# A fused attention and Mish block: raw weight loads gated by an estimate of when their buffer was read, and the first correction rows turned and moved in one piece

## The chip, the cores and the metric

One core of one Trainium2 chip. The time is that of one execution on the device in microseconds (us); of several runs the median is given. The core has five engines with queues of their own, each of which runs its instructions in order: PE (matrix products), ACT (scalar functions, and copies out of the product banks), DVE (vector work), POOL (vector work in on-chip memory only) and SP (which here only issues transfers). A transfer is issued on one of these queues and then runs on 16 DMA engines. An instruction that waits holds everything behind it on its queue.

## The reference

```
xn = layernorm(x)                                      # x: 2048 rows of 512
q = (xn @ wq) as 32 heads of 16;  k = xn @ wk;  v = xn @ wv   # one key and value head for all
s = softmax(q k^T / 4) v, heads side by side, @ wo
h = xn @ w1 + b1                                       # 1792 hidden features
g = silu( (h * tanh(softplus(h))) @ w2 )
out = x + s * g
```

All arrays are float32, and the weights are drawn large, so the softmax is kept stable by subtracting the greatest score of each row.

## The kernel before

**Precision.** Products that need nearly full precision are made of three with operands that are split into a high and a low part (`mm12`, L645: 3 products for each 128 of the inner size). So each weight tile is loaded raw (`raw...`, 128x512), its high part is rounded out by ACT or POOL, and POOL subtracts to get the low part (`split`, L456). There are two raw buffers for all weights (`RAWS`, L424). The split form is then stored once to DRAM (`keep`, L475) and loaded again ready made for later row blocks. `ws` names the tiles of w1, `wb` those of w2 and wo, `wq` those of wq; in the lead-in the first `ws` tiles live in `xtw`.

**Work.** The rows are done in four blocks of 512 (`c`). A query step `v` is a group of four heads of one block: 32 steps. For each, a first set of score products `m` (L1054), 64 of them, is reduced by DVE to the greatest score of each row (L1058, `mb`). From these `c_rows` (L1070) makes two correction rows in four parts: `reduce` (L1077), `parts` (L1080 and L1082), `turn` (a transpose, L1087) and `move` (eight small transfers, L1097), which put the rows into the query tile `qt`. Then the score products `e` (L1025) come out with the maximum already subtracted, ACT takes the exponential (L1030, `pts`) and PE multiplies by the values (L1112, `pv`). Between these, the products of the other matrices run in groups of 12 or so into a bank `xps`: projections of q (copied out at L723 as `qf`), the hidden layer (L778, `hb`, then three ACT functions and POOL products into `act`), and the second layer and wo (`wbs`).

**Order.** The whole order is written out by the program, without any automatic scheduling. The main part runs in steps: 16 for each `v`, four `e` each, and four steps form a unit with one `xps` group (L653) in half-height products (L116). The lead-in, before the first `e`, is a small planner (L1393 to L1474): tasks with an engine, an estimated duration and dependencies are taken in the order of their estimated start, with clocks `T` for each engine. The main part is expected to begin at `E0` = 81 us of this plan. Where PE has nothing ready, the planner puts in pieces of an `xps` group at full height (L112) or a warming product (`warm`, L1348). `c_rows(0)`, the rows of the first query step, is three DVE tasks and an SP task there (L1433 to L1444).

**Loads.** `load` (L491) queues the raw load of the next tile on SP as soon as fewer than two raw tiles are taken in the plan, and `split` gives a raw tile free when the split has been written into the order (`raws[0] -= 1`, L468). `pool_at` and `busy` hold the planner's estimate of when POOL is done with what was given to it, and `step_of` turns it into steps. A load that is queued into a raw tile waits on SP until POOL's subtraction has read it.

**Key moves.** The keys of block c are copied, their low part made (L169, `ks`), and half of them are moved to the other partitions by `k_move` (L349, transfers at L351). The first score products against these keys wait for that.

Of the kernel before, what the change touches and what calls it, by code (L numbers as in the profile page):

```python
# [122 lines left out]
def block_kernel(ctx: ExitStack, tc: tile.TileContext, x, wq, wk, wv, wo, w1, b1, w2, out):  # L123
# [21 lines left out]
    def step_of(us):  # L145
        return base[0] + (us - base[1]) / STEP_US
# [34 lines left out]
    def f(ap):  # L181
        return ap.bitcast(F32)
# [199 lines left out]
    for j in range(4):  # L382
        o = slice(DH * j, DH * (j + 1))
# [38 lines left out]
    RING = {"wq": 1, "ws": 2, "wb": 5, "wx": 4}  # L422
    NRAW = {"wq": 1, "ws": 1, "wb": 1, "wx": 1}
    RAWS = 2  # L424
    raws = [0]
    items = {t: [] for t in RING}
    todo = {t: [0, 0] for t in RING}
    queue = deque()
# [27 lines left out]
    def split(tag):  # L456
        k = todo[tag][0]
        it = items[tag][k]
        w = home(tag, k)
        if not lead:  # L460
            busy[0] = max(busy[0], us_of(it.step + 1))
        if lead:
            act.activation(w[:, 0], it.raw, AF.Copy)
        else:
            hi_pool(w[:, 0], it.raw)
        sub(pool, w[:, 1], it.raw, f(w[:, 0]))
        it.tile, it.ready = w, pool_at(0.2)
        raws[0] -= 1  # L468
        todo[tag][0] += 1
        keep(it)  # L470

# [19 lines left out]
    def load(tag):  # L491
        its = items[tag]
        k, n = todo[tag]
        if tag == "wx" and m1_done.get((NC - 2, NFT - 1)) is None or lead and tag == "wq" and n > 1:
            return
        if n == len(its):
            return
        it = its[n]
        if taken(tag, n) and (tag != "ws" or kept.get(it.key)):
            return  # L500
        if n == k and kept.get(it.key):
            it.tile = home(tag, n)
            sp.dma_start(f(it.tile), kept[it.key])
            it.ready = math.ceil(2 * (sp_at(0.5) + 1.6)) / 2
            todo[tag][:] = n + 1, n + 1
        elif n - k < NRAW[tag] and raws[0] < RAWS:
            r = sb.tile([P, D], F32, tag="raw", name=f"raw{tag}{n}", bufs=RAWS)
            if len(it.src.shape) == 3:
                sp.dma_start(r.rearrange("p (t n) -> p t n", t=NDT), it.src)
            else:  # L510
                sp.dma_start(r, it.src)
            it.raw, it.step = r, (lead["arrive"]() if lead else sp_at(0.45))
            raws[0] += 1
            todo[tag][1] += 1

    def pump():
# [553 lines left out]
    def c_rows(v):  # L1070

        mp = sb.tile([P, 2, 3, 8], F32R, tag="mp", name=f"mp{v}", bufs=2)
        mx = f(mp[:, :, 0])
        w = {}

        def reduce():
            dve.reduce_max(out=mx, in_=mb_of[v].rearrange("p b (a z) -> p a z b", a=2), axis=AX.X)  # L1077

        def parts():
            dve.tensor_reduce(out=mp[:, :, 1], in_=mx.rearrange("p a (z o) -> p a z o", o=1), axis=AX.X,  # L1080
                              op=ALU.max, negate=True)
            dve.tensor_reduce(out=f(mp[:, :, 2]), in_=f(mp[:, :, 0:2]).rearrange("p a s z -> p a z s"), axis=AX.X,  # L1082
                              op=ALU.add, negate=True)

        def turn():
            cr = w["cr"] = sb.tile([P, 32], F32, tag="cr", name=f"cr{v}", bufs=2)
            dve.transpose(cr, f(mp[:, :, 1:3]).rearrange("p a s z -> p a (s z)"))  # L1087

        def move():
            q, cr = qt_of[v], w["cr"]  # L1090
            if not lead:
                sp_t[0] = max(sp_t[0], us_of(step[0]) + 4.0)
            for a in range(1, -1, -1):
                r = 64 * a + 48
                for b in range(4):
                    sp_at(0.68)
                    (act if lead and b % 2 else sp).dma_start(f(q[r:r + 2]).rearrange("o p (t b n) -> b o (p t) n", b=4, n=32)[b],  # L1097
                                 cr[32 * b + 16 * a:32 * b + 16 * a + 16])
        return reduce, parts, turn, move

# [105 lines left out]
    now = [0.0]  # L1206
# [15 lines left out]
    def task(eng, us, fn, deps=(), **kw):  # L1222
        t = Task(eng, us, fn, deps, **kw)
        plan[eng].append(t)
        return t
# [161 lines left out]
                   for d in k.deps)  # L1387

    begun = [0]
    rows = []  # L1390
    cdone = [None]
    kind = [None]
    while True:  # L1393
# [7 lines left out]
        b = best("PE")  # L1401
# [13 lines left out]
        s, e, k = min(opts, key=lambda o: o[0])  # L1415
# [5 lines left out]
        if k == "M":  # L1421
# [11 lines left out]
            if vdone[0] == 0 and got[0] == 32 and m_next[0] == m_next[1]:  # L1433
                vdone[0] = 1
                r = c_rows(0)
                r0 = task("DVE", 0.26, r[0])
                rp = task("DVE", 0.3, r[1], [r0])
                r1 = task("DVE", 0.25, r[2], [rp])
                rows[:] = [r0, rp, r1]

                def move():
                    r[3]()
                    cdone[0] = now[0] + 2 * 0.65 + 2.0
                task("SP", 2.6, move, [r1])  # L1444
        elif k == "X":
            fresh = cur["g"] is None
            if cur["g"] is not None or not waiting and (vdone[0] or begun[0] < 1 + (s - 18) / X_US) and begin():
# [149 lines left out]
```

## Time and profile before

| | |
|---|---|
| median of 3 runs | 1586.17 us (1585.98 to 1589.31) |
| the profiled execution's own time | 1585.09 us |
| its span, first to last instruction | 1583.3 us |
| PE busy | 1563.0 us |
| DVE, ACT, POOL busy | 1333.4, 1297.2, 638.5 us |
| mean granted clock of PE | 0.997 |
| first half-height product (begin of the main part) | 90.72 us |

All rows are from that one execution; times in rows are from the start of its span. A row of the timeline gives start, duration, engine, line, operation and tiles; in brackets stands how long the engine was idle before it and what ended that. `x4` is a merged run of four. `SPq` and `ACTq` are instructions that issue transfers. Rows of stretches give busy time and count for PE, PEld (weight loads), DVE, ACT and POOL, then the granted clock, the busy share of the DMA engines and GB/s.

### The profile page before, as it was taken

The page shows a single profiled execution, that of the slowest core. Times are in us where ns is not written, and L with a number is a line of the kernel's source. Part 1 is how long each engine was busy: PE and PEld are TensorE (multiplying, and loading weights), DVE is VectorE, ACT ScalarE, POOL GpSimd, SP SyncE. Part 2 cuts the span into 40 slices and gives each one's busy share as a digit, 9 for nine tenths or more (in the row PEclk, how much of TensorE's full clock was granted, in tenths as well). Part 3 has the DMA queues.
Part 4 walks back from the last instruction along what each step waited for, and adds up shares of the span by engine and source line. Part 5 has one row for each costly group of instructions (what it writes and reads, how often), then busy time and mean ns, then how long its engine had stood idle before and what let it go on. Part 6 is the DMA issues. An engine that isn't in the chain of part 4 may idle for free.

```text
span 1583.3 us, 31336 instructions
## 1 busy us (share of the span) xinstructions
PE 1563.0 (99%) x11682; PEld 880.2 (56%) x11682; DVE 1333.4 (84%) x2275; ACT 1297.2 (82%) x2511; POOL 638.5 (40%) x672
## 2 busy tenths in 40 slices
PE   9899999999999999999999999999999999999998
PEld 6455555655555565565555556556555555655643
DVE  7888888888988988888998988888889999888821
ACT  6479789878898778877988888897788978888796
POOL 4677349438267111431624422163152323315021
PEclk9999999999999999999999999999999999999999
DMA  6332134124052213203114230322322213031200
GB/s 209 95 132 85 30 110 130 51 67 168 23 157 64 73 56 111 64 22 103 55 29 138 89 94 16 103 68 79 100 59 60 81 55 114 16 97 32 74 21 27
DMA packets 74375, 124.94 MB, mean 79 GB/s; under 512 B 21536, under 2 KB 36160, under 8 KB 74224
## 3 DMA queue, kind: packets, MB, share of 16 engines
q1 hardware_dynamic: 74152, 122.94, 25.2%
q8 instruction: 93, 1.52, 0.4%
q14 instruction: 58, 0.48, 0.1%
q10 hardware_dynamic: 72, 0.01, 0.0%
HBM read 75.05 MB, written 26.21 MB: 64 GB/s over the span
## 4 chain that ended last, share of the span: by engine, by line
PE 93%; ACT 2%; POOL 2%; DVE 1%; DMA 1%; issue 0%; SPq 0%; ACTq 0%; DVEq 0%; POOLq 0%
PE xps L116 41%; PE pv L1112 31%; PE m L1054 12%; PE e L1025 6%; PE xps L112 1%; ACT pts L1030 1%; DMA rawwb<-in_dram 1%; PE warm L1269 1%; DVE mb L1058 0%; POOL wbs L169 0%; PE wop L112 0%; PE warm L1348 0%; DMA ks<-ks 0%; PE kp L335 0%; POOL u L169 0%
## 5 line engine op out<-in xcount | busy, mean ns | idle before, releaser
L1058 DVE TENSOR_REDUCE mb<-m 128x1 f32<-128x512 f32 x2048 | 1266.0, 682 | 178.4 <-PE m L1054 158.8
L1030 ACT ACTIVATE pts<-e 128x512 f32<-128x512 f32 x2042 | 1062.5, 606 | 220.3 <-PE e L1025 147.9
L1054 PE MATMUL m<-ks,qt 48*128 48x512 f32 (+1 forms) x2048 | 841.8, 425 | 4.8 <-DMA ks<-ks 4.3
L1025 PE MATMUL e<-qt,ks 64*128 64x512 f32 x2048 | 748.0, 407 | 2.2 <-ACT pts L1030 2.1
L1112 PE MATMUL pv<-pts,vaug 128*32 128x512 f32 x4084 | 531.0, 603 | 0.0
L1054 PEld LDWEIGHTS m<-ks,qt 48*128 48x128 f32 (+1 forms) x2048 | 368.1, 185 | 110.3 <-DVE mb L1058 53.2
L1025 PEld LDWEIGHTS e<-qt,ks 64*128 64x128 f32 x2048 | 372.5, 186 | 29.9 <-ACT pts L1030 19.3
L116 PE MATMUL xps<-wbs,act 64*128 64x512 f32 x1248 | 315.2, 397 | 0.0
L116 PE MATMUL xps<-xt,ws 64*128 64x512 f32 x1128 | 312.9, 410 | 0.5 <-ACT pts L1030 0.5
L116 PEld LDWEIGHTS xps<-xt,ws 64*128 64x128 f32 x1128 | 194.8, 185 | 182.8 <-ACT pts L1030 120.7
L116 PEld LDWEIGHTS xps<-wbs,act 64*128 64x128 f32 x1248 | 226.1, 185 | 65.4 <-ACT pts L1030 33.5
L1112 PEld LDWEIGHTS pv<-pts,vaug 128*32 128x32 f32 x4084 | 87.8, 108 | 150.4 <-issue 142.5
L169 POOL TENSOR_TENSOR hb<-hb,t 128x512 f32<-128x512 f32 x56 | 72.2, 1289 | 149.1 <-PE m L1054 72.4
L179 POOL TENSOR_SCALAR t<-t 128x512 f32<-128x512 f32 x56 | 34.5, 616 | 173.7 <-ACT t L784 173.6
L116 PE MATMUL xps<-xt,wq 64*128 64x512 f32 x336 | 92.9, 409 | 0.0
L116 PEld LDWEIGHTS xps<-xt,wq 64*128 64x128 f32 x336 | 57.9, 185 | 54.8 <-ACT pts L1030 37.7
L169 POOL TENSOR_TENSOR oc<-oc,sc 128x512 f32<-128x512 f32 (+1 forms) x16 | 20.6, 1288 | 147.5 <-DMA wbs<-w 71.3
L116 PE MATMUL xps<-wbs,ot_all 64*128 64x512 f32 x288 | 79.5, 408 | 0.0
L116 PEld LDWEIGHTS xps<-wbs,ot_all 64*128 64x128 f32 x288 | 49.5, 184 | 47.1 <-ACT pts L1030 29.3
L169 POOL TENSOR_TENSOR act<-hb,act 128x512 fp32r<-128x512 f32 x56 | 72.3, 1291 | 4.7
L169 POOL TENSOR_TENSOR hb<-hb,u 128x512 f32<-128x512 f32 x56 | 72.3, 1292 | 4.4
L169 POOL TENSOR_TENSOR u<-u,t 128x512 f32<-128x512 f32 x56 | 72.0, 1286 | 4.7
(146 smaller groups left out, 878.1 us busy)
## 6 DMA issues: line engine op xcount, KB each, us to landing
wbs<-w SPq DMA_DIRECT2D x38, 512.0 KB
ws<-w SPq DMA_DIRECT2D x34, 512.0 KB
qt<-qh SPq DMA_DIRECT2D x256, 32.0 KB
w<-wbs SPq DMA_DIRECT2D x14, 512.0 KB
wq<-wq SPq DMA_DIRECT2D x14, 512.0 KB
w<-ws SPq DMA_DIRECT2D x12, 512.0 KB
wbs<-wo SPq DMA_DIRECT2D x12, 512.0 KB
rawws<-in_dram SPq DMA_DIRECT2D x22, 256.0 KB
```

Of the source, the lines that this page charges most:

```text
L112: self.pe.matmul(ps, self.lhs(), self.rhs(), start=(self.k == 0), stop=(self.k == self.tot - 1))
L116: i = self.pe.matmul(ps, self.lhs()[o], self.rhs()[o], start=(self.k == 0 and self.halves == 0), stop=(self.k == self.tot - 1 and self.hal ...
L169: eng.tensor_tensor(out=o, in0=a, in1=b, op=op)
L179: pool.tensor_scalar(o, o, lim, 0.0, op0=ALU.min, op1=ALU.max)
L1025: pe.matmul(e, ks[o:o + 64, P * k:P * (k + 1)], q[o:o + 64, p], start=True, stop=True)
L1030: x = act.activation(dst, e, AF.Exp, scale=0.25)
L1054: pe.matmul(m, q[o, p, P * t:P * (t + 1)], ks[o, C * kb:C * (kb + 1)], start=True, stop=True)
L1058: return dve.reduce_max(out=mb_of[v][:, kb, z:z + 1], in_=m, axis=AX.X)
L1112: pe.matmul(o[32 * j:32 * j + 32], vaug[:, k], pt, start=(k == 0), stop=(k == 15))
L1269: pe.matmul(warm, qts[0][:, 0, 0:P], qts[0][:, 0], start=True, stop=True)
```

## The change

Three edits. A raw load is queued only if the raw tile that has been free longest is estimated to have been read by POOL (a list `freed` of such times takes the place of the counter), with a tolerance of 0.1 steps in the lead-in and 0.8 afterwards; a step is 2.88 us. The eight first-row transfers of the lead-in are all issued by SP, instead of by SP and ACT in turn. And the three DVE parts of these rows are one task of the planner, so nothing comes between them; the planner's price of the move goes from 2.6 to 5.2 us, and the time from which the main part may begin from two to four issues (0.65 us each) and 2 us after the move's start.

```
-    raws = [0]
+    freed = deque([-10.0 ** 6] * RAWS)
...
         it.tile, it.ready = w, pool_at(0.2)
-        raws[0] -= 1
+        freed.append(step_of(busy[0]))
...
-        elif n - k < NRAW[tag] and raws[0] < RAWS:
+        elif n - k < NRAW[tag] and freed and freed[0] <= step[0] + (0.1 if lead else 0.8):
+            freed.popleft()
...
-            raws[0] += 1
...
-                    (act if lead and b % 2 else sp).dma_start(f(q[r:r + 2])...
+                    sp.dma_start(f(q[r:r + 2])...
...
-                r0 = task("DVE", 0.26, r[0])
-                rp = task("DVE", 0.3, r[1], [r0])
-                r1 = task("DVE", 0.25, r[2], [rp])
-                rows[:] = [r0, rp, r1]
+                r1 = task("DVE", 0.9, lambda: (r[0](), r[1](), r[2]()))
...
-                    cdone[0] = now[0] + 2 * 0.65 + 2.0
-                task("SP", 2.6, move, [r1])
+                    cdone[0] = now[0] + 4 * 0.65 + 2.0
+                task("SP", 5.2, move, [r1])
```

PE's instructions stand in the same order in both, apart from one warming product of the lead-in that is gone. DVE's differ only in the place of the row parts. The queues of SP, ACT and POOL differ in the lead-in and in the first two row blocks; after that they are the same.

SP in the lead-in, before; `xtk` is a copy of the normalized rows to DRAM, `ks` the keys, `qt0` the first query step, `cr0` its turned rows:

```order
L947 DMA xtk3_673<-xf3_0_611 128x1024
L509 DMA rawws3_680<-in_5_dram 128x4x128
L947 DMA xtk3_673<-xf3_1_612 128x1024
L511 DMA rawwb2_693<-in_7_dram 128x512
L509 DMA rawws4_753<-in_5_dram 128x4x128
L351 DMA ks_92<-ks_92 48x256 x2
L511 DMA rawwb3_791<-in_7_dram 128x512
L509 DMA rawws5_802<-in_5_dram 128x4x128
L509 DMA rawws6_898<-in_5_dram 128x4x128
L509 DMA rawws7_940<-in_5_dram 128x4x128
L1097 DMA qt0_77<-cr0_952 2x8x32 x4
```

and now:

```order
L947 DMA xtk3_673<-xf3_0_611 128x1024
L947 DMA xtk3_673<-xf3_1_612 128x1024
L510 DMA rawws3_697<-in_5_dram 128x4x128
L512 DMA rawwb2_711<-in_7_dram 128x512
L351 DMA ks_92<-ks_92 48x256 x2
L510 DMA rawws4_806<-in_5_dram 128x4x128
L510 DMA rawws5_884<-in_5_dram 128x4x128
L1097 DMA qt0_77<-cr0_878 2x8x32 x8
L510 DMA rawws6_936<-in_5_dram 128x4x128
L512 DMA rawwb3_986<-in_7_dram 128x512
```

The last key move now stands ahead of `rawws4`, the row transfers, now eight, stand ahead of `rawws6` and `rawwb3`, and `rawws7` has moved further back.

ACT at the end of the lead-in, before; `hb` is the eviction of a hidden-layer bank, L463 a split, L793 and L797 functions of the hidden layer:

```order
L778 ACTIVATE hb0_3_930<-xps_891,b1c_100 128x512
L463 ACTIVATE xtw_128<-rawws6_898 128x512
L1097 DMA qt0_77<-cr0_952 2x8x32 x4
L778 ACTIVATE hb0_4_983<-xps_948,b1c_100 128x512
L463 ACTIVATE xtw_128<-rawws7_940 128x512
```

and now:

```order
L778 ACTIVATE hb0_3_934<-xps_891,b1c_100 128x512
L463 ACTIVATE wbs_101<-rawwb2_711 128x512
L793 ACTIVATE t0_1_793<-u0_1_794,two_86 128x512
L778 ACTIVATE hb0_4_978<-xps_950,b1c_100 128x512
L797 ACTIVATE t0_1_793<-t0_1_793 128x512
```

Ahead of `hb0_4` stand a split and a logarithm, and no transfer.

DVE at the rows of the first step, before; `mp0` holds the row maxima and their parts, `mb1` is the next step's maxima:

```order
L1077 TENSOR_REDUCE mp0_880<-mb0_372 128x2x8
L1058 TENSOR_REDUCE mb1_767<-m1_0_2_900 128x1
L1058 TENSOR_REDUCE mb1_767<-m1_1_2_903 128x1
L1058 TENSOR_REDUCE mb1_767<-m1_0_3_906 128x1
L1058 TENSOR_REDUCE mb1_767<-m1_1_3_909 128x1
L1080 TENSOR_REDUCE mp0_880<-mp0_880 128x2x8
L1082 TENSOR_REDUCE mp0_880<-mp0_880 128x2x8
```

and now:

```order
L1077 TENSOR_REDUCE mp0_874<-mb0_372 128x2x8
L1080 TENSOR_REDUCE mp0_874<-mp0_874 128x2x8
L1082 TENSOR_REDUCE mp0_874<-mp0_874 128x2x8
L1087 STREAM_TRANSPOSE cr0_878<-mp0_874 128x32
L1058 TENSOR_REDUCE mb1_763<-m1_0_2_895 128x1
```

The turn (L1087) stood behind four more reductions before, eight behind L1077; now it follows L1082.

More of the change, by code (lines that the diff above doesn't have):

```diff
@@ L1096, in move @@
                     sp_at(0.68)
-                    (act if lead and b % 2 else sp).dma_start(f(q[r:r + 2]).rearrange("o p (t b n) -> b o (p t) n", b=4, n=32)[b],
+                    sp.dma_start(f(q[r:r + 2]).rearrange("o p (t b n) -> b o (p t) n", b=4, n=32)[b],
                                  cr[32 * b + 16 * a:32 * b + 16 * a + 16])
@@ L1389, in block_kernel @@
     begun = [0]
-    rows = []
     cdone = [None]
```

## The prediction

> **What bounds the kernel now.** I read the page first (engine shares, the chain), then stretches of busy time, then the chain in the one stretch where PE isn't full, and last the four engines' rows there.
>
> ```profile
> PE 1563.0 (99%) x11682; PEld 880.2 (56%) x11682; DVE 1333.4 (84%) x2275; ACT 1297.2 (82%) x2511; POOL 638.5 (40%) x672
> PE 93%; ACT 2%; POOL 2%; DVE 1%; DMA 1%; issue 0%; SPq 0%; ACTq 0%; DVEq 0%; POOLq 0%
> ```
>
> PE carries the end: it is busy for 99% of the span and holds 93% of the chain. By stretches (PE, PEld, DVE, ACT, POOL busy, then the granted clock):
>
> ```profile
> 46.00:58.00 12.00, 12.00 (x62) 6.42 (x60) 11.94 (x22) 5.70 (x14) 7.98 (x8) 1.00 0.54 177
> 58.00:64.00 6.00, 1.59 (x7) 0.91 (x7) 2.29 (x4) 2.07 (x4) 3.28 (x4) 1.00 0.36 101
> 64.00:76.00 12.00, 10.54 (x40) 5.85 (x36) 9.81 (x16) 3.60 (x7) 10.12 (x11) 0.86 0.09 23
> 76.00:83.00 7.00, 6.88 (x32) 4.23 (x31) 6.41 (x15) 1.57 (x3) 6.13 (x6) 1.00 0.13 40
> 83.00:92.00 9.00, 6.57 (x27) 4.09 (x26) 5.54 (x10) 3.19 (x6) 4.98 (x5) 0.81 0.32 94
> 92.00:100.00 8.00, 6.89 (x44) 3.58 (x43) 7.61 (x14) 6.97 (x14) 4.33 (x5) 1.00 0.19 73
> ...
> 100.00:125.00 25.00, 25.00 (x196) 13.31 (x189) 21.85 (x39) 22.51 (x44) 23.46 (x25) 1.00 0.44 150
> ...
> 350.00:375.00 25.00, 24.54 (x188) 12.80 (x185) 21.80 (x39) 21.63 (x43) 18.81 (x20) 1.00 0.46 158
> ...
> 1475.00:1500.00 25.00, 25.00 (x201) 15.02 (x196) 21.33 (x36) 17.52 (x35) 0.00 (x0) 1.00 0.22 70
> ```
>
> From 100 to 1500 us PE is full (the first and the last of 56 rows of 25 us stand here, and the only one with a gap, 0.46 us). The change leaves PE's instructions there in the same order, so what is saved or lost in the lead-in passes to the end undiminished, as long as no operand comes late. What can move is in 58 to 100 us: PE idles 4.41 + 1.46 + 0.12 + 2.43 + 1.11 = 9.53 us there, and the clock is below 1 in two of the stretches. The chain at the first gap:
>
> ```profile
> 58.62 1.29 POOL xtw L169
> 59.91 0.02 issue
> 59.93 0.38 SPq L509
> ...
> 60.40 0.52 SPq L351
> 60.92 0.05 issue
> 60.97 2.48 DMA ks<-ks
> ```
>
> POOL's subtraction for raw weights `ws3` ends at 59.91; only then may SP queue `rawws4` into the raw tile it frees (L509, 59.93), and behind that instruction stands the move of the last key block (L351), whose landing PE waits for. PE's rows and DVE's:
>
> ```profile
> 58.98 0.97 PE L112 MATMUL xps<-xt,wq 128*128 128x512 f32 x3 [0.78 <-ACT hb L778]
> 63.58 0.90 PE L1054 MATMUL m<-ks,qt 64*128 64x512 f32 x4 [3.63 <-DMA ks<-ks]
> 64.41 2.93 PE L112 MATMUL xps<-xt,wq 128*128 128x512 f32 x6
> ...
> 71.28 1.65 PE L112 MATMUL xps<-xt,xtw 128*128 128x512 f32 x6
> ...
> 82.20 1.67 PE L112 MATMUL xps<-xt,ws 128*128 128x512 f32 x6
> 86.31 0.50 PE L1348 MATMUL warm<-qt 128*128 128x512 f32 x1 [2.43 <-ACT hb L778]
> ...
> 90.72 0.62 PE L116 MATMUL xps<-xt,ws 64*128 64x512 f32 x1
> ```
>
> ```profile
> 54.53 0.85 DVE L169 TENSOR_TENSOR ks<-kp,ks 16x256 fp32r<-16x256 f32 x2
> ...
> 67.94 2.48 DVE L1058 TENSOR_REDUCE mb<-m 128x1 f32<-128x512 f32 x4 [1.38 <-PE m L1054]
> ...
> 79.10 0.16 DVE L1080 TENSOR_REDUCE mp<-mp 128x16 fp32r<-128x16 f32 x1
> 79.29 0.19 DVE L1082 TENSOR_REDUCE mp<-mp 128x16 f32<-128x32 f32 x1
> ...
> 82.02 0.20 DVE L1087 STREAM_TRANSPOSE cr<-mp 128x32 f32<-128x32 f32 x1
> ...
> 87.27 2.48 DVE L1058 TENSOR_REDUCE mb<-m 128x1 f32<-128x512 f32 x4 [2.69 <-PE m L1054]
> 90.53 7.26 DVE L1058 TENSOR_REDUCE mb<-m 128x1 f32<-128x512 f32 x12 [0.78 <-PE m L1054]
> ```
>
> The reader is to see two holes in both engines, at 60 and at 84 us. The second has another cause, ACT:
>
> ```profile
> 82.25 3.20 ACTq L1097 DMA_DIRECT2D qt<-cr  x4
> 85.56 0.69 ACT L778 ACTIVATE hb<-xps,b1c 128x512 f32<-128x512 f32 x1 [4.83 <-DMA qt<-cr]
> ```
>
> ACT issues four of the eight first-row transfers and holds the eviction of PE's bank (`hb0_4`) behind them; PE, done at 83.87 (82.20 + 1.67), waits until 86.31.
>
> **The parts and their cost.**
>
> *Key move past the raw load.* In the new order of SP, `rawws4` stands behind the key move, and only `rawwb1`, `rawws3` and `rawwb2`, which were ahead of it before too, precede it. So the move no longer waits for POOL at 59.91 but for its own operand, DVE's L169, which ends at 54.53 + 0.85 = 55.38. In the old trace the chain needs 63.58 − 60.40 = 3.18 us from the issue to PE's start; so 58.6. PE isn't there yet: its three products end at 58.98 + 0.97 = 59.95. Gain 63.58 − 59.95 = 3.63 us; what is late next is PE itself. Bounds: 0 if SP is still held, 3.63 at most.
>
> *The slow clock behind the first gap.* One microsecond of each stretch:
>
> ```profile
> 65.00:66.00 1.00, 1.00 (x4) 0.80 (x3) 1.00 (x3) 0.56 (x1) 0.92 (x3) 0.50 0.00 0
> ...
> 89.00:90.00 1.00, 1.00 (x4) 0.35 (x5) 0.76 (x2) 0.00 (x0) 1.00 (x2) 0.50 0.39 110
> ```
>
> Behind each hole the granted clock is half for some 3 us. The six products at 64.41 take 2.93 us against 1.65 for six at full clock (71.28): 1.28 us, and DVE's idle 1.38 us before 67.94 says PE was the one awaited. Without the gap: 1.3 us gained, bounds 0 and 1.38.
>
> *First rows' transfers off ACT.* `hb0_4` no longer stands behind four issues. ACT gets there with a split and a logarithm ahead of it whose inputs are old, so the eviction follows PE's last product at once. PE also loses one warming product (0.50). DVE sets the limit: it idles 2.69 us before 87.27 and carries the same reductions, so of PE's 2.43 + 0.50 = 2.93 us no more than 2.69 is gained; I take 2.6 (bounds 0, if ACT is late for another reason, and 2.69). Behind that hole the half clock returns (88.4 to 91.4 by rows of 1 us like the second above), and DVE waits 0.78 us before 90.53: 0.6 of it gained (bounds 0 and 0.78).
>
> By the Trainium skill (TensorE: Matmul & The Clock Gate, Part 1), the clock falls to half after an idle window of about 3.4 us. The 3.63 us hole agrees; the half clock behind 2.43 us of idling is more than that rule predicts from the hole alone. By the rule the second slow stretch would have another cause and stay, and the time would be 0.6 us above mine.
>
> *Eight transfers on SP.* They cost SP:
>
> ```profile
> 82.86 2.99 SPq L1097 DMA_DIRECT2D qt<-cr  x4
> ```
>
> that is 0.75 us each, 6.0 us for eight, where before four ran beside ACT's four. Queued behind them are `rawws6`, `rawwb3` and the next head's query rows. What hides them: the rows are turned in one piece, right behind L1077, and so ahead of the eight reductions that stood between (2 × 2.48 = 4.96 us). The turn ends at 82.02 + 0.20 − 4.96 − 3.63 − 1.3 = 72.3; the last issue ends at 78.3; with 2.48 us to land, as for the keys, 80.8. The first score product needs them behind PE's lead-in, whose end moves from 90.72 by 8.1 to 82.6. Margin 1.8 us, so cost 0 (bounds 0, and 3.0 if the four issues saved on ACT's queue come back in full on SP's). The reductions pushed behind the turn start 0.16 + 0.19 + 0.20 us later, and the same instructions are gone further on: 0.
>
> By the Trainium skill (DMA: Bandwidth & Descriptors, Issuing engines are not separate DMA queues), spreading transfers over engines saves nothing but issue time. That speaks against this part: the saved issue time is what is given up, and if the rows came last, the whole would be 1581.
>
> *Loads queued later.* Two splits fewer are done in the lead-in (`ws7`, and one of `wb`), and POOL does them later, at 23.46 of 25 us busy. For `ws7`: between the split of `ws6` and the end of its own POOL has 9 products or subtractions and 8 scalings,
>
> ```profile
> 107.46 0.62 POOL L164 TENSOR_SCALAR xtw<-rawws 128x512 fp32r<-128x512 f32 x1
> 108.16 1.28 POOL L169 TENSOR_TENSOR xtw<-rawws,xtw 128x512 fp32r<-128x512 f32 x1
> ...
> 113.62 0.69 ACT L778 ACTIVATE hb<-xps,b1c 128x512 f32<-128x512 f32 x1
> ```
>
> 9 × 1.28 + 8 × 0.70 (start to start in the first two rows) = 17.1 us from about 84.6 (estimate: `hb0_1`'s three products and the split of `ws6`, 4.6 us, from ACT's exponential at 80): 101.7. PE needs `ws7` when `hb0_6` is evicted, 113.62 − 90.72 = 22.9 us into the main part: 105.5. Margin 3.8 us; cost 0, bounds 0 and, if POOL slips by a whole hidden-layer piece (four instructions, 3.9 us), 0.1. Later loads come to PE's order several steps ahead of use, and where they wait now (SP behind POOL) they wait less: 0.
>
> **Sum.** 3.63 + 1.3 + 2.6 + 0.6 = 8.1 us off the profiled execution's own 1585.09 us (span 1583.3): 1577.0. The median shown, 1586.17, is 1.1 above that execution, so 1578.1 for a median.
>
> **Rivals.**
>
> *Only the first hole closes.* ACT's new order or DVE's backlog holds the second where it is: gain 3.63 + 1.3 = 4.9, 1581.2. For it: DVE is busy 6.41 of 7 us from 76 to 83, so little room is there to come earlier. Against: DVE idles 2.69 us in that hole.
>
> *Rows last.* The eight transfers on SP end the lead-in: `rawws5` stands ahead of them and waits for POOL's split of `ws4`. If this split ends later than 74.1 (72.3 + the margin), the score products slip by as much; I work it out at 68.1 (query split, 2 us, and its own subtraction, 1.28, from 64.8). 1580 to 1582.
>
> *Late weights, the slower side.* With fewer splits done ahead, POOL at 94% is the bound of the first units and PE waits at `ws7`. Each microsecond past 105.5 costs one; it takes 8.1 us of it to eat the gain, so `ws7` ready at 113.6, and 3.2 more to be measurably slower, about 1590. For it: 23.46 of 25. Against: 3.8 us of margin, and PE asks for one weight tile only every 22.9 / 2 = 11.5 us.
>
> *The change doesn't do it.* The estimate of when a raw tile is free runs ahead of POOL and SP is held as now: 1586. Against: in the new order the load that held SP stands behind the key move.
>
> **How the numbers follow.** Forecast 0.72, only the first hole 0.12, rows last 0.06, late weights 0.06, no effect 0.04. About 0.2% (3.2 us) is what a measurement of this kernel can tell from no change. Faster: 0.72 + 0.12 + 0.06 = 0.90, and 0.01 from late weights that eat only part; same 0.04; slower 0.05. The bounds of the gain are 3.63 (1582.5) and 9.53 of idling plus the half clocks, 0.14 × 12 + 0.19 × 9 = 3.4 us, together 12.9 (1573.3); for 8 in 10 I take 1574.5 to 1582.5, which holds the first three cases.
>
> **What would show it.** The key move issued near 55.4; no PE wait over 1 us on `ks`; the clock at 1.00 throughout 58 to 92; ACT's `hb0_4` within 0.1 us of PE's last product; the first L116 product near 82.6; PE full from 100 us on. It is wrong if SP's raw loads wait long ahead of the key move or of the rows, if the first score product waits for `qt<-cr`, or if PE waits for POOL at `ws7`.

## The result, and the profile after

The changed kernel takes 1579.05 us in the median of five runs (1575.9 to 1579.4), the kernel before 1589.31 us (1585.98 to 1591.67) on the same chip: a ratio of 0.9933, with a 95% interval of 0.9914 to 0.9952. By that ratio it is 10.6 us faster, by the interval 7.6 to 13.7. The profiled execution took 1576.23 us, 8.86 less than the one profiled before.

The page of the changed kernel, engines and chain:

```profile
PE 1559.7 (99%) x11681; PEld 876.0 (56%) x11681; DVE 1333.2 (85%) x2275; ACT 1295.0 (82%) x2509; POOL 636.8 (40%) x672
PE 96%; ACT 2%; DVE 1%; DMA 0%; POOL 0%; issue 0%; DVEq 0%; POOLq 0%; ACTq 0%
```

DMA and POOL, which held 1% and 2% of the chain, hold next to none of it now. The stretches of the lead-in, with the columns as before:

```profile
58.00:64.00 6.00, 5.22 (x25) 2.83 (x22) 5.18 (x10) 2.97 (x5) 5.03 (x6) 1.00 0.14 40
64.00:76.00 12.00, 10.42 (x44) 5.88 (x44) 10.98 (x22) 4.03 (x7) 11.30 (x12) 1.00 0.09 24
76.00:83.00 7.00, 6.83 (x34) 4.34 (x33) 7.00 (x13) 3.72 (x7) 4.93 (x5) 1.00 0.25 79
83.00:92.00 9.00, 8.02 (x50) 3.79 (x48) 9.00 (x16) 7.29 (x14) 8.60 (x9) 1.00 0.50 168
...
350.00:375.00 25.00, 25.00 (x196) 13.42 (x194) 21.77 (x37) 22.42 (x43) 17.39 (x18) 1.00 0.31 99
```

The granted clock is 1.00 in all of them; DVE is busy for all of 76 to 92 us; and the gap of 0.46 us between 350 and 375 is gone as well. PE's rows that answer to those before, and its last one:

```profile
55.05 1.66 PE L112 MATMUL xps<-xt,xtw 128*128 128x512 f32 x6 [0.88 <-ACT hb L778]
...
59.96 0.97 PE L112 MATMUL xps<-xt,wq 128*128 128x512 f32 x3 [0.78 <-ACT hb L778]
60.86 0.74 PE L1054 MATMUL m<-ks,qt 64*128 64x512 f32 x4
61.52 1.67 PE L112 MATMUL xps<-xt,wq 128*128 128x512 f32 x6
...
77.94 1.67 PE L112 MATMUL xps<-xt,ws 128*128 128x512 f32 x6
80.44 1.64 PE L1348 MATMUL warm<-qt 128*128 128x512 f32 x6 [0.17 <-ACT hb L778]
82.59 0.39 PE L116 MATMUL xps<-xt,ws 64*128 64x512 f32 x1
...
1564.13 4.46 PE L112 MATMUL wop<-wbs,ot_all 128*128 128x512 f32 x18
```

The product on the last keys (60.86) waits for nothing, the six behind it take 1.67 us instead of 2.93, and in front of the last warming products stand 0.17 us of waiting instead of 2.43. At 55.05 stands a wait of 0.88 us that the profile before doesn't have. What PE waited for stands earlier on SP, and the rows are turned ahead of the reductions on DVE:

```profile
55.16 1.16 SPq L351 DMA_DIRECT2D ks<-ks  x2
...
72.78 5.37 SPq L1097 DMA_DIRECT2D qt<-cr  x8
```

```profile
72.50 0.21 DVE L1087 STREAM_TRANSPOSE cr<-mp 128x32 f32<-128x32 f32 x1
72.64 2.44 DVE L1058 TENSOR_REDUCE mb<-m 128x1 f32<-128x512 f32 x4
75.35 16.89 DVE L1058 TENSOR_REDUCE mb<-m 128x1 f32<-128x512 f32 x28 [0.27 <-PE m L1054]
```

**One scale for all traces.** The row at 59.96, three products of `wq` behind the eviction of `hb0_1`, is in every kernel here the last one ahead of the first hole, and PE's work ahead of it is the same (but for the last two kernels of the table, which have a few products more). It stood at 58.98 before, but further runs of nearly the same code put it anywhere from 58.95 to 63.63. So I count from this mark. Before, the last products began at

```profile
1572.95 4.48 PE L112 MATMUL wop<-wbs,ot_all 128*128 128x512 f32 x18
```

1572.95 − 58.98 = 1513.97 us behind the mark; now it is 1564.13 − 59.96 = 1504.17. The change gained 9.80 us behind the mark, and the profiled execution shows 8.8 of its span because it reached the mark 0.98 later. All traces on this scale, in us:

| kernel | mark | first L116 product behind mark | last products behind mark | against before |
|---|---|---|---|---|
| before | 58.98 | 31.74 | 1513.97 | |
| the change | 59.96 | 22.63 | 1504.17 | −9.80 |
| gate alone | 59.14 | 27.84 | 1508.09 | −5.88 |
| rows alone | 62.84 | 28.66 | 1511.04 | −2.93 |
| change, rows as three tasks | 63.63 | 24.72 | 1505.17 | −8.80 |
| change, transfers on SP and ACT | 59.10 | 23.72 | 1505.05 | −8.92 |
| before, first hole filled | 60.04 | 30.46 | 1513.30 | −0.67 |
| before, second hole filled | 59.41 | 31.21 | 1513.29 | −0.68 |
| change, 7 us more on POOL | 58.95 | 22.63 | 1507.87 | −6.10 |
| change, half a store later | 62.46 | 22.63 | 1504.08 | −9.89 |
| change, both halves later | 61.20 | 22.64 | 1505.48 | −8.49 |
| change, stores doubled | 60.04 | 28.29 | 1509.85 | −4.12 |
| change, 5 products in the first keys' wait | 60.80 | 22.62 | 1504.26 | −9.71 |
| change, 3 products there and half a store later | 59.70 | 22.64 | 1503.41 | −10.56 |

Behind the mark the kernels with half a store later and with 3 products besides are the same program, and yet their last column differs by 0.67 us, with no idle time of PE to show for it. So differences of less than about 0.7 us between single traces say nothing there.

### The profile page after: what moved, and what is told of

It reads as the page before. It is cut to its first block, busy times and chain, and to the rows that moved or that the text cites. A ratio compares the mean times of both kernels' runs of the same rounds, so it can differ in the third digit from the quotient of the medians.

```text
span 1574.5 us, 31330 instructions
## 1 busy us (share of the span) xinstructions
PE 1559.7 (99%) x11681; PEld 876.0 (56%) x11681; DVE 1333.2 (85%) x2275; ACT 1295.0 (82%) x2509; POOL 636.8 (40%) x672
## 4 chain that ended last, share of the span: by engine, by line
PE 96%; ACT 2%; DVE 1%; DMA 0%; POOL 0%; issue 0%; DVEq 0%; POOLq 0%; ACTq 0%
PE xps L116 43%; PE pv L1112 31%; PE m L1054 11%; PE e L1025 6%; PE xps L112 2%; ACT pts L1030 1%; DVE mb L1058 1%; PE warm L1269 1%; PE kp L335 0%; PE wop L112 0%; PE xp L294 0%; PE warm L1348 0%; DMA rawwb<-in_dram 0%; DMA ks<-ks 0%; ACT hb L778 0%
## 5 line engine op out<-in xcount | busy, mean ns | idle before, releaser
L116 PE MATMUL xps<-wbs,act 64*128 64x512 f32 x1248 | 315.2, 397 | 0.0
L116 PE MATMUL xps<-xt,ws 64*128 64x512 f32 x1128 | 313.3, 410 | 0.3 <-ACT pts L1030 0.3
L116 PEld LDWEIGHTS xps<-xt,ws 64*128 64x128 f32 x1128 | 194.5, 185 | 183.4 <-ACT pts L1030 121.4
L116 PEld LDWEIGHTS xps<-wbs,act 64*128 64x128 f32 x1248 | 225.9, 185 | 66.4 <-ACT pts L1030 32.7
L1112 PEld LDWEIGHTS pv<-pts,vaug 128*32 128x32 f32 x4084 | 87.8, 108 | 151.1 <-issue 143.1
L116 PE MATMUL xps<-xt,wq 64*128 64x512 f32 x336 | 93.0, 409 | 0.0
L116 PEld LDWEIGHTS xps<-xt,wq 64*128 64x128 f32 x336 | 57.9, 185 | 55.2 <-ACT pts L1030 37.7
L116 PE MATMUL xps<-wbs,ot_all 64*128 64x512 f32 x288 | 79.3, 408 | 0.0
L116 PEld LDWEIGHTS xps<-wbs,ot_all 64*128 64x128 f32 x288 | 49.5, 184 | 46.9 <-ACT pts L1030 28.5
```

What stands on the lines that cost most here:

```text
L116: i = self.pe.matmul(ps, self.lhs()[o], self.rhs()[o], start=(self.k == 0 and self.halves == 0), stop=(self.k == self.tot - 1 and self.hal ...
L1112: pe.matmul(o[32 * j:32 * j + 32], vaug[:, k], pt, start=(k == 0), stop=(k == 15))
```

## The experiments

### The gate alone, and the rows alone

The first takes the rows' part out of the changed kernel:

```
-                    sp.dma_start(f(q[r:r + 2])...
+                    (act if lead and b % 2 else sp).dma_start(f(q[r:r + 2])...
...
-                r1 = task("DVE", 0.9, lambda: (r[0](), r[1](), r[2]()))
+                r0 = task("DVE", 0.26, r[0])
+                rp = task("DVE", 0.3, r[1], [r0])
+                r1 = task("DVE", 0.25, r[2], [rp])
...
-                task("SP", 5.2, move, [r1])
+                task("SP", 2.6, move, [r1])
```

> The changed kernel with the eight first-row transfers again shared by SP and ACT and the rows again three separate DVE tasks, so that only the gate on the raw loads is left. Theory (two holes with two causes): the key move is issued near 55, the first hole and the half clock behind it are gone (gain about 4.3 us at that place, as in the changed kernel), the second hole of some 2 us in front of hb0_4 stays with the half clock behind it; first half-height product at 86.0 to 86.8 us, time 1581 to 1582 on the scale where before is 1585 to 1586. Rival (one cause: the late key move makes everything behind it late, and the second hole closes with the first): first half-height product near 83, time as the changed kernel's.

1580.84 us in the median (1579.33 to 1583.64), ratio 0.9954 (0.994 to 0.9967). PE in its trace:

```profile
59.14 0.97 PE L112 MATMUL xps<-xt,wq 128*128 128x512 f32 x3 [0.78 <-ACT hb L778]
60.70 1.67 PE L112 MATMUL xps<-xt,wq 128*128 128x512 f32 x6
...
77.10 1.67 PE L112 MATMUL xps<-xt,ws 128*128 128x512 f32 x6
81.23 0.79 PE L1348 MATMUL warm<-qt 128*128 128x512 f32 x1 [2.46 <-ACT hb L778]
86.98 0.62 PE L116 MATMUL xps<-xt,ws 64*128 64x512 f32 x1
```

and ACT:

```profile
77.17 3.22 ACTq L1097 DMA_DIRECT2D qt<-cr  x4
80.49 0.69 ACT L778 ACTIVATE hb<-xps,b1c 128x512 f32<-128x512 f32 x1 [3.90 <-DMA qt<-cr]
```

The first hole is gone, the second stands as it did before (2.46 against 2.43 us), behind ACT's four issues. The two holes have two causes; the rival with one cause falls. The half clock behind the second hole lasted 6.8 us here instead of 3.4, so that from the last six products to the first L116 product it took 86.98 − 77.10 = 9.88 us, 1.4 more than before.

The second run puts the rows' part alone into the kernel before (the same lines the other way; raw loads queued as before).

> The kernel before with the rows' part of the change alone: all eight transfers on SP, the three row parts one DVE task; raw loads queued as before. Theory: the 3.6 us hole in front of the last keys and its slow clock stay (first product of the last keys near 63.6), the second hole closes; first half-height product 86.4 to 87.2 us, time 1581 to 1582 on the scale where before is 1585 to 1586; the gains of this run and of the gate alone add up to that of the changed kernel, 8.1 us. Rival: with SP held by raw loads the eight transfers on SP land last and the first score product waits for qt<-cr: first half-height product at 89 or later.

1584.74 us (1582.08 to 1586.81), ratio 0.9974 (0.9964 to 0.9984). PE:

```profile
62.84 0.97 PE L112 MATMUL xps<-xt,wq 128*128 128x512 f32 x3 [0.78 <-ACT hb L778]
67.43 1.31 PE L1054 MATMUL m<-ks,qt 64*128 64x512 f32 x4 [3.62 <-DMA ks<-ks]
68.67 2.93 PE L112 MATMUL xps<-xt,wq 128*128 128x512 f32 x6
...
86.83 1.67 PE L112 MATMUL xps<-xt,ws 128*128 128x512 f32 x6
89.34 1.65 PE L1348 MATMUL warm<-qt 128*128 128x512 f32 x6 [0.17 <-ACT hb L778]
91.50 0.39 PE L116 MATMUL xps<-xt,ws 64*128 64x512 f32 x1
```

Here the first hole stays and the second closes; PE doesn't wait for `qt<-cr`, so the rival with the rows last falls. From the last six products to the first L116 product it takes 91.50 − 86.83 = 4.67 us, as in the changed kernel (82.59 − 77.94 = 4.65); before it took 90.72 − 82.20 = 8.52. So the second hole with all behind it was worth 3.87 us. The first one, counted from the mark to the group behind it (69.73 − 58.98 = 10.75 before, 65.44 − 59.96 = 5.48 after), was worth 5.27. My expectation that both runs add up to 8.1 was too simple: −5.88 and −2.93 make 8.81 of 9.80. In the run with the rows alone, too, the half clock lasted 6.8 us instead of 3.4, here behind the first hole, which took 0.76 us back; why, is seen below. By the medians the two are 8.1 and 4.2 us below the kernel before of their series (1588.91), which is more than the whole change; with a start that scatters by 3 us or more, medians of five to twelve runs don't divide the gain that finely.

### Which of the rows' two edits

The changed kernel with the three DVE tasks again (the lines with `r0`, `rp` and `r1` above, the move still all on SP), and with SP and ACT in turn again (the line of `dma_start` above and the move's price).

> The changed kernel with the rows as three separate DVE tasks again; all eight transfers stay on SP. Theory (the hole is closed by taking the transfers off ACT, and the one piece only lets the rows land in time): no wait of hb0_4 on qt<-cr, no second hole in PE, but the rows are turned about 5 us later than in the changed kernel (near 77.5), the last of eight issues ends near 83 and lands near 85.5, so the first score product waits for qt<-cr for up to 3 us; first half-height product 83 to 86. Rival (the one piece closes the hole): the hole in front of hb0_4 stays though ACT issues nothing.

1580.9 us in one execution. DVE and SP:

```profile
81.42 0.20 DVE L1087 STREAM_TRANSPOSE cr<-mp 128x32 f32<-128x32 f32 x1
```

```profile
81.69 5.37 SPq L1097 DMA_DIRECT2D qt<-cr  x8
```

PE's wait in front of `hb0_4` is 0.84 us, not 2.46 as with the gate alone, so taking the transfers off ACT closes most of the hole by itself; what is left is the eviction, which starts 0.09 us behind PE's last product (83.36 against 83.27). The rows are turned 17.8 us behind the mark, 5.3 later than in the changed kernel (12.5), as expected. The wait for `qt<-cr` that I expected doesn't appear: the planner now begins the main part later and puts three full-height products of its first group ahead of it. So the first L116 product came 2.1 us later and the end only 1.0.

> The changed kernel with the eight transfers shared by SP and ACT again; the rows stay one piece. Theory: turned at 72.5 the rows are ready before ACT comes to its four issues, so these cost ACT their issue time (4 x 0.67 = 2.7 us) and no wait; the eviction of the bank ahead of or behind them comes up to 2.7 us later and PE waits there by at most 2 us; first half-height product 82.6 to 84.6. Rival (ACT's four issues are hidden, since ACT has slack of about 3 us there): first half-height product at 82.6, the transfers off ACT are worth nothing once the rows are early.

1576.28 us in one execution. ACT and PE:

```profile
75.14 0.69 ACT L778 ACTIVATE hb<-xps,b1c 128x512 f32<-128x512 f32 x1 [2.93 <-DMA qt<-cr]
```

```profile
75.88 1.66 PE L112 MATMUL xps<-xt,ws 128*128 128x512 f32 x6 [1.19 <-ACT hb L778]
```

Issued early, ACT's four transfers still hold an eviction, now that of `hb0_3`, and PE waits 1.19 us; the end comes 0.88 later. So either edit of the rows alone, added to the gate (5.88), gives most of what the second hole is worth (8.80 and 8.92 of 9.80). What the two together add shows in PE's waits of 0.84 and 1.19 us; at the end it is 0.9 to 1.0 us, little more than two traces of one program differ by.

### The half clock behind the holes

In the kernel before, products whose results nobody reads fill one hole each; the wait itself stays.

```
+        if lead and (v, n, a) == (0, 24, 0):
+            for i in range(13):
+                w = ps_m.tile([P, C], F32, tag="m", name=f"fill{i}")
+                pe.matmul(w, qts[2][:, 0, 0:P], qts[2][:, 0], start=True, stop=True)
```

(the second run: 9 of them ahead of the product that waits for `hb0_4`).

> The kernel before with 13 extra products, whose results nobody reads, ahead of the first product of the last keys: they fill the 3.6 us in which PE waited. Theory (the half clock of 64 to 67 us is the consequence of that idle time): granted clock 1.00 in 64 to 67, the six products there take 1.65 instead of 2.93 us, and everything behind comes 1.2 to 1.4 us earlier: first half-height product near 89.4. Rival (the half clock has another cause): clock 0.50 and 2.93 us as before, first half-height product at 90.7 or later.

PE and one stretch:

```profile
64.57 0.73 PE L1058 MATMUL m<-ks,qt 64*128 64x512 f32 x4 [0.50 <-DMA ks<-ks]
65.24 1.66 PE L112 MATMUL xps<-xt,wq 128*128 128x512 f32 x6
```

```profile
64.00:68.00 4.00, 3.50 (x17) 2.14 (x17) 2.92 (x5) 2.40 (x4) 3.00 (x4) 1.00 0.33 103
```

Clock 1.00, 1.66 us for the six, and the first L116 product 1.28 us earlier on the scale of the mark (30.46 against 31.74): as expected, and the predicted 1.3. By the end half of it is gone again (−0.67). At the evictions of the hidden layer (L778) it is still 1.1 us some 180 us behind the mark and 0.85 at 980, and PE idles about as long on the way as before, so it goes in the kind of scatter that the table shows.

> The kernel before with 9 extra products, whose results nobody reads, ahead of the product that waits for hb0_4: they fill the 2.43 us hole near 84 us, and the first hole stays. Theory (the half clock of 88.4 to 91.4 follows from this hole): granted clock 1.00 there, first half-height product 0.5 to 0.8 us earlier, near 90.0. Rival (DVE, which waits for PE there, or ACT sets the end): the clock is 1.00 but the first half-height product stays at 90.7. Second rival: by the Trainium skill (TensorE: Matmul & The Clock Gate, Part 1) an idle window of about 3.4 us is needed, so this hole would not be the cause and the half clock would stay.

The stretch behind the first hole, which is open here, and that behind the filled second one:

```profile
62.00:69.00 7.00, 5.01 (x14) 2.94 (x14) 2.57 (x5) 2.40 (x4) 4.51 (x5) 0.51 0.39 119
...
83.00:92.00 9.00, 8.91 (x41) 5.23 (x37) 6.30 (x13) 3.57 (x6) 4.42 (x5) 1.00 0.24 63
```

The second half clock is gone. In the three traces that have this hole of 2.4 us (before, gate alone, before with the first hole filled) it is there; in the other eleven no half clock begins between 76 and 92 us. So the hole was its cause, against the rule weighed in the prediction (the Trainium skill, TensorE: Matmul & The Clock Gate, Part 1), which asks for about 3.4 us of idling. The first L116 product comes 0.53 us earlier by the mark, although the first hole, 3.62 us as before, now had nearly 7 us at half clock behind it instead of 3.4 and lost 0.59 more: from the group behind the first hole (70.75) it is 90.62 − 70.75 = 19.87 us against 90.72 − 69.73 = 20.99, a gain of 1.1.

Cut into tenths of a microsecond, the half clocks of the traces stand so:

| trace | PE idle | clock at 0.50 | length |
|---|---|---|---|
| before, first hole | 59.95 to 63.58 | 64.2 to 67.6 | 3.4 |
| before, second hole | 83.87 to 86.31 | 88.1 to 91.5 | 3.4 |
| before with the first filled, second hole | 83.31 to 85.75 | 86.0 to 89.4 | 3.4 |
| before with the second filled, first hole | 60.37 to 63.99 | 62.1 to 68.9 | 6.8 |
| rows alone, first hole | 63.81 to 67.43 | 65.9 to 72.7 | 6.8 |
| gate alone, second hole | 78.77 to 81.23 | 80.9 to 87.8 | 6.8 |

The length is one or two times 3.4 us, and the start isn't tied to the hole: it falls into it or up to 1.8 us behind it. Inside one trace the starts are whole multiples of 3.41 us apart (64.2 and 88.1 before: 23.9 = 7 × 3.41; 28.4 and 65.9 with the rows alone: 11 × 3.41). By the Trainium skill (TensorE: Matmul & The Clock Gate, Part 1), activity is judged in windows of 3413 ns that run free of the program; the lengths and spacings here agree. In these six rows the half clock lasts 6.8 us where it starts inside the hole, and 3.4 where it starts behind it. So, as far as they show, the same hole costs one window or two by where it falls among them.

A hole isn't always needed: in the trace of the change with both halves of a store later the clock is at half from 93.6 to 97.0, and in the 8 us ahead of that, at the start of the main part, PE's longest waits are 0.47, 0.30 and 0.50 us. In another trace a wait of 1.19 us at 75 us brought none. What decides in such cases stays open. That kernel's row in the table (−8.49) lies 1.4 us behind that of the one with half a store later, and it is there that it falls behind.

### What late weights cost

In the changed kernel ten repeats of the scaling ahead of `ws7`'s subtraction:

```
             hi_pool(w[:, 0], it.raw)
+            for _ in range(10 if (tag, k) == ("ws", 7) else 0):
+                pool.tensor_scalar(w[:, 0], it.raw, 1.0, 0.0, op0=ALU.mult, op1=ALU.add)
```

> The changed kernel with the scaling of ws7's high part done eleven times on POOL instead of once, with the same result each time: 10 x 0.70 = 7.0 us more work in front of ws7's subtraction. It prices the late weights. Theory (ws7 is ready 2.5 us before PE needs it): ws7's subtraction ends near 109.8 instead of 102.8, PE waits for it by about 4.5 us, and the last products end 3.5 to 4.5 us later than in the changed kernel. Rival (POOL's order gives the time back, or PE's order finds no wait): less than 1 us later.

POOL and PE:

```profile
99.78 0.62 POOL L164 TENSOR_SCALAR xtw<-rawws 128x512 fp32r<-128x512 f32 x1
100.49 6.93 POOL L467 TENSOR_SCALAR xtw<-rawws 128x512 fp32r<-128x512 f32 x10
107.50 1.28 POOL L169 TENSOR_TENSOR xtw<-rawws,xtw 128x512 fp32r<-128x512 f32 x1
```

```profile
107.47 0.71 PE L116 MATMUL xps<-xt,xtw 64*128 64x512 f32 x1 [1.99 <-POOL xtw L467]
...
108.83 0.79 PE L116 MATMUL xps<-xt,xtw 64*128 64x512 f32 x1 [0.22 <-POOL xtw L169]
```

PE reached `ws7` at 107.47 − 1.99 = 105.48. Without the repeats the high part would have been there at 99.78 + 0.62 = 100.40, so the margin is 5.1 us, and 7.0 us more on POOL give 2.2 us of waiting. But the end comes 3.70 us later: behind the wait the clock is at half from 107.6 to 111.0 (3.4 us), which adds the rest. I expected 4.5 us of waiting and 3.5 to 4.5 at the end: the price was right, its parts weren't.

### The wait at 55 us

In the changed kernel both 512 KB halves of a store (`xtk3`) are issued together behind `rawwb1`, whose split on ACT stands ahead of `hb0_0`, which PE waits for there. First, one half of the store is issued later:

```
+                if (c, k) != (3, 1):
                     task("SP", 0.5, keep_x, xs, prio=2)
...
         moved = task("SP", 1.0 if c else 0.5, mv, [kl])
...
+        if c == 3:
+            task("SP", 0.5, keep_x, xs + [moved], prio=2)
```

> The changed kernel with the second half of the last xtk store (512 KB) issued behind the last key move instead of together with the first half. Theory (the two stores together slow rawwb1's transfer from 3.24 to 4.17 us, and ACT's split, hb0_0 behind it and PE wait for it): rawwb1 takes about 3.2 us, PE's wait of 0.88 us near 55 on hb0_0 is gone or under 0.2, the first product of the last keys starts near 60.0 instead of 60.86, first half-height product near 81.7 instead of 82.59; time 0.5 to 1 us less than the changed kernel. Rival (the slow transfer has another cause): rawwb1 takes about 4.2 us as before and nothing moves. Second rival (DVE, busy without a break from 72.6, sets the end of the lead-in): the wait at 55 goes, first half-height product stays near 82.5.

1576.02 us (1575.12 to 1578.64), ratio 0.9922 (0.9909 to 0.9936), which overlaps that of the change. The wait is gone in its trace, but so it was in two of the four traces of kernels without the gate, which have one half of the store there, and in the other two it was 0.38 and 0.99. So the change needn't be its cause. The first L116 product, which I expected 0.9 us earlier, stands at 22.63 us behind the mark as in the changed kernel. With both halves later, and with the stores doubled (`for _ in range(2 if c == 3 else 1)` around the store):

> The changed kernel with both 512 KB halves of the last xtk store issued behind the last key move, so that no store runs beside rawwb1's load. From rawwb1's issue to the split that waits for it took 3.68 to 4.19 us in the five traces with both halves together behind it and 3.26 to 4.31 us in the five with one half. Theory (the stores slow the load): under 3.0 us, no PE wait on hb0_0 in front of the six products near 54. Rival (its duration has nothing to do with the stores): 3.3 to 4.3 us as in the others.

> The changed kernel with each half of the last xtk store written twice (four stores of 512 KB behind rawwb1's issue instead of two). Theory (the stores slow the load): over 4.5 us from rawwb1's issue to the split, PE's wait on hb0_0 1.2 us or more, and the key move, behind two more issues on SP, not later than its operand. Rival: 3.7 to 4.2 us, as with two stores, since the load is issued first and ahead of them.

From `rawwb1`'s issue to the landing of its last part it took 3.37 us with no store beside it, 3.24 to 4.29 in seven traces with one, and 3.47 to 4.17 in six with two. The theory that the stores slow it expected under 3.0 without them, and that falls; one store gave both the shortest and the longest time. The doubled stores are no test of it: only the first of the four was issued while the load ran (3.54 us; it counts with the seven), the second at 54.07, behind the split. What makes this load take 3.2 us in one execution and 4.3 in another stays open; it is worth 0 to 1 us.

The doubled stores showed something else. SP, what it waited for from 48 to 60 us (in all, times, longest), and PE:

```profile
49.69 8.67 SPq L948 DMA_DIRECT2D xtk<-xf  x4
...
59.83 1.15 SPq L351 DMA_DIRECT2D ks<-ks  x2
```

```profile
SPq L948 <- DMA xtk<-xf: 6.7, 2, 3.5
```

```profile
64.28 1.31 PE L1055 MATMUL m<-ks,qt 64*128 64x512 f32 x4 [3.27 <-DMA ks<-ks]
```

Two stores took SP 1.21 us in the changed kernel, four took 8.67. The issues aren't longer (0.32 to 0.37 us each in both): the second copy of a half goes to the same place as the first, and SP waits until the first has landed, twice for nearly 3.5 us. Against my expectation the last key move then stood behind these waits until 59.83, as it stood behind `rawws4` until 60.40 before, and the first hole was back: 3.27 us, half clock behind it, 5.7 us at the end. That the hole comes from a transfer that waits ahead of the key move on SP is so shown twice, with two different transfers and two different waits.

### Where a spread of 3 us comes from

The times of the changed kernel lie at 1575.9 and 1576.2, and at 1579.1 to 1579.4; the mean granted clock of the lower two is 1.000 and 0.999, that of the upper three 0.997 to 0.998. The trace of the changed kernel is that of a lower one; that of a neighbour shows what a lower clock can come from. In the trace with half a store later PE's rows at the start of the lead-in, and its stretches:

```profile
25.95 0.47 PE L1054 MATMUL m<-ks,qt 64*128 64x512 f32 x1 [1.01 <-DMA ks<-ks]
26.36 0.98 PE L335 MATMUL kp<-xf,wkf 128*64 128x256 f32 x4
```

```profile
20.00:26.00 6.00, 4.95 (x32) 3.48 (x29) 2.79 (x6) 5.47 (x16) 2.43 (x9) 1.00 0.25 59
26.00:34.00 8.00, 8.00 (x29) 3.20 (x30) 4.00 (x7) 4.88 (x12) 1.60 (x4) 0.57 0.53 173
```

PE waits 1.01 us for the first moved keys and then runs at half clock for 6.8 us; the mark came at 62.46. In the traces where this wait was 0.38 to 0.69 us, and in one with 0.75, the clock stayed at 1.00; where it was 1.01, 1.05 or 1.28, and in one with 0.73, half clock followed for 3.4 to 10.3 us and the mark came at 61.2 to 63.6. Products put into this wait, in the changed kernel:

```
+        if lead and (v, n, a) == (0, 0, 1):
+            for i in range(5):
+                w = ps_m.tile([P, C], F32, tag="m", name=f"fill{i}")
+                pe.matmul(w, qts[2][:, 0, 0:P], qts[2][:, 0], start=True, stop=True)
```

> The changed kernel with 5 extra products, whose results nobody reads, ahead of the first product that waits for the first moved keys (near 24.5 us). In the traces so far PE waits there for 0.38 to 1.28 us, and in those where it waits over 1 us (the run with the rows' part alone, the one with three DVE tasks, the one with the later store) the clock is at half for 3.4, 10.3 and 6.8 us behind it and the three products of wq (the mark that stands at 59 to 60 us in the others) come at 62.5 to 63.6. Theory (this wait, through the clock, makes the two groups of times some 3 us apart): the clock is 1.00 from 20 to 45 us, the mark stands at 59 to 60.5, and the times of five runs lie within 1.5 us of each other, near the lower group of the changed kernel (1576). Rival (the start differs for another reason, the landing of the inputs): times spread over 3 us as before. Second rival: the five products come late themselves and cost their 1.15 us in every run.

Five runs between 1576.68 and 1577.20 us, a spread of 0.52 instead of 3.5, ratio 0.9931 (0.9917 to 0.9944). The stretch in its trace:

```profile
20.00:45.00 25.00, 24.91 (x129) 13.83 (x126) 17.36 (x30) 19.84 (x55) 9.41 (x23) 1.00 0.43 135
```

The mark stands at 60.80, later than where the clock stayed up without them, and all five times lie 0.5 to 1.3 us above the lower two of the changed kernel, so the second rival (the products cost time themselves) holds in part. With three of them, and half a store later:

> The changed kernel with the second half of the last xtk store behind the last key move, and 3 extra products (about 0.7 us at full clock) in PE's wait for the first moved keys. Theory (that wait, through the clock, makes the upper group of times, and five products were more than was needed): five times within 1.5 us of each other, between 1575.0 and 1576.7, median 0.5 to 1.5 us below the run with five products (1577.19) and below the changed kernel's median (1579.05). Rival (three products leave enough idle time for the clock to fall in some runs): one or more times near 1578 to 1579 with a mean clock of 0.997 or 0.998.

Six runs between 1575.09 and 1576.16, median 1575.64, ratio 0.9924 (0.9911 to 0.9937). In its median it is 3.4 us below the changed kernel's, measured in another series, and 12.4 below the kernel before on its own; the ratios to the kernel before overlap. What is shown is that the upper times are gone, in eleven runs of two kernels with these products, where three of the changed kernel's five were upper ones.

## Why the prediction was right, and where it was off

**Key move past the raw load** and **the slow clock behind the first gap**: 3.63 + 1.3 = 4.93 predicted, 5.27 measured from the mark to the group behind the hole. The key move was issued at 55.16 (predicted 55.4), and PE reached the keys without a wait. The gate alone gives this, and the filled hole shows that the clock was worth 1.28. In the profile of after the product on the last keys came only 2.72 us earlier, at 60.86 instead of 59.95, since PE reached the mark 0.98 late; that belongs to the start, which differs by as much or more between executions.

**First rows' transfers off ACT**: 2.6 + 0.6 = 3.2 predicted, 3.87 measured. The step that was off is the cap by DVE: I allowed no more than DVE's idle time at two rows (2.69 and 0.78), but DVE was also idle for 0.59 of 76 to 83 us (busy 6.41 of 7), and all of that went: it is busy without a break from 76 to 92 now. The prediction also gave the whole of this gain to the transfers; the turn in one piece, which it counted only as cover for the eight issues, gives most of it as well (8.92 of 9.80 with the transfers still shared).

**Eight transfers on SP**: cost 0 predicted, and no product waits for `qt<-cr`. They were issued from 72.78 to 78.15, 0.67 us each instead of the 0.75 assumed; rows that land last showed nowhere. With the turn 5.3 us later they didn't either, but there the planner began the main part 2.1 us later.

**Loads queued later**: cost 0 predicted, with 3.8 us of margin at `ws7`; 5.1 were there. The rule in the rival of late weights, that each microsecond past the margin costs one, is wrong: 2.2 us of waiting cost 3.7, because the clock falls behind it. And the cost was below 0: the gap of 0.46 us between 350 and 375 is open in the three other kernels without the gate, too (0.15 to 1.22 us at 365), and closed in all ten with it. PE waits there for ACT's exponential, and ACT, ahead of that, for POOL (rows of before):

```profile
357.18 0.62 POOL L164 TENSOR_SCALAR wbs<-rawwb 128x512 fp32r<-128x512 f32 x1 [3.06 <-DMA rawwb<-in_dram]
...
363.83 0.72 ACT L793 ACTIVATE t<-u,two 128x512 f32<-128x512 f32 x1 [1.09 <-POOL u L169]
```

POOL was late because it had waited 3.06 us for a raw load, and SP had issued that load at 354.14, when POOL's subtraction of the tile before ended (354.12). In the trace of the change POOL's longest wait for a raw load between 336 and 358 us is 0.99 us, and L793 waits for nothing.

Together 9.80 us behind the mark against 8.1 predicted, so the sum was 1.7 too small: 0.3 and 0.7 in the two holes, and 0.7 behind the first L116 product. Of these 0.7, 0.6 are there by the ninth eviction of the hidden layer (78.03 us behind the mark before, 68.30 now); the half clock before ran on to 91.5, beyond that product. The gap adds 0.5, and about as much is lost again up to the end, with no idle time of PE in either trace. That the first L116 product stood at 82.59, where 82.6 was forecast, is luck: it came 9.1 us earlier by the mark instead of 8.1, and the mark 0.98 later. The predicted 1578.1 lies 0.95 below the measured median because two errors cancel: the medians are 10.26 apart instead of 8.1, and the kernel before came to 1589.31 in these runs where I started from 1586.17.

The rivals: only the first hole closes, rows last, and no effect are excluded by the rows above; late weights needed 7 us of extra work to appear. The rule on the clock (second half clock stays) fell when the second hole was filled, and when it was closed: the clock of the changed kernel is 1.00 from 58 to 92.

## What to carry to other kernels

A load that waits for its buffer holds every transfer behind it on an in-order queue, and so does a store that waits for another to land; whatever an engine waits for next must stand ahead of it, which is decided where the load is queued, not where its data is needed. Price a hole in PE with the clock behind it: here 2 to 3.6 us of idling brought 3.4 or 6.8 us at half speed with it. Compare traces from a common row, not from the start of the span, when the start itself varies by more than the effect.

## What was unexpected about the hardware

The half clock came in pieces of 3.4 us on a beat of its own, so that one and the same hole cost one piece or two, and a wait of 1.0 us in the early lead-in brought 6.8 us of it. A wait of 2.0 us in the middle of a stretch where PE was otherwise full was enough for one piece, and once, at the start of the main part, a piece came with no wait over 0.5 us ahead of it. And one and the same load of 256 KB took 3.24 us to land in one execution and 4.29 in another, with one store beside it in both.
